# Loading w1 and w2 in chunks of 4, 4, 4 and 2 tiles, and a residual add with a choice of engine, in a fused scan and MLP kernel

## The chip, the core and the metric

The kernel runs on one core of a Trainium2 chip. The metric is the device time of one execution in microseconds (us), lower is better. A core has five engines that matter here: TensorE (PE in the profile; PEld is its weight load), VectorE (DVE), ScalarE (ACT), GpSimd (POOL) and SyncE (SP), which in this kernel issues nearly all transfers between the chip's main memory (DRAM) and the on-chip memory (SBUF). TensorE writes its products into PSUM, which has eight banks. Each engine works through its own list of instructions in order and waits on semaphores for the others.

## The reference, cut to what matters

One sequence of 2048 rows with 448 channels goes through a layer norm, a diagonal complex linear recurrence over time ("A"), and beside it through a small MLP with a hidden width of F = 1792 ("B"). The MLP's output gates the recurrence, and x is added at the end.

```python
def _A_ref(x, Lambda_re, Lambda_im, B_re, B_im, C_re, C_im, log_dt, Dskip):
    ...
    Lam_bar = jnp.exp(dt * Lam)
    Bu = jnp.einsum("bld,pd->blp", x + 0j, B_bar)
    for t in range(L):
        h = Lam_bar[None, :] * h + Bu[:, t, :]
        hs.append(h)
    hseq = jnp.stack(hs, 1)
    return 2.0 * jnp.einsum("blp,dp->bld", hseq, Cmat).real + x * Dskip[None, None, :]

def _B_ref(x, w1, b1, w2, b2):
    y = _layernorm(x, axis=-1)
    h = _gelu(jnp.einsum("bsd,df->bsf", y, w1) + b1)
    return jnp.einsum("bsf,fd->bsd", h, w2) + b2

x = A_x
xn = _layernorm(x, axis=-1)
s = _A_ref(xn, ...)
g = _silu(_B_ref(xn, B_w1, B_b1, B_w2, B_b2))
return x + s * g
```

All inputs and the output are bf16.

## The kernel before

The rows of x come in 8 blocks of 256 rows (even and odd rows of a block side by side, `par` 0 and 1), two blocks to a group, four groups. The recurrence is worked out on pairs of rows, with a scan on VectorE. For each group TensorE does: products with B (`bu`, L613), with w1 (`mm1`, L683; for the first group in halves of 256 columns, `mm1_half`, L699), with w2 (`mm2`, L714), and with C (`ym`, L746, L749 and L752). Small products (`m0`, L602 and L604) prepare a matrix once. The layer norm of a group is worked out by VectorE and either GpSimd or VectorE, and its result is transposed by DMA (`xnT` for the recurrence, `xn2T` for the MLP); only the first group's MLP input is transposed on TensorE (L379, L437).

The program is a list of tasks with what each reads and writes. Two lists of numbers fix the order in which the tasks are emitted, and which tasks with a choice of two engines take the second. Both lists were made beforehand; the kernel holds only their result.

```python
ORDER = [int(k) for k in """
0 11 18 22 12 1 9 10 19 23 14 83 16 20 24 17 2 15 5 21 25 13 27 3 26 7 8 85 6 28 4 86 29 91 40 87 30 92 84 88 93 31 89 41 94 32 43 42 44 90 48 97 95
# ... cut: 625 numbers in all
""".split()]
SECOND = [int(k) for k in """
138 141 142 143 167 171 173 197 199 217 223 284 311 318 320 393 395 396 421 422 424 425 428 503 505 506 507 532 534 535 538 541 603
""".split()]
```

The loads, issued by SyncE in this order (L84 is the helper's line):

```python
NW1 = 2

def ldw1(c, prio):
    w = F // NW1
    ld("sp", w1_sb[:, 0:3, c * w:(c + 1) * w],
       dram_ap(B_w1, c * w, [[F, 128], [128 * F, 3], [1, w]]), [f"w1_{c}"], 384 * w * 2, prio, dur=0.55)
    ld("sp", w1_sb[0:64, 3, c * w:(c + 1) * w], dram_ap(B_w1, 384 * F + c * w, [[F, 64], [1, w]]),
       [f"w1r_{c}"], 64 * w * 2, prio)

for par in range(2):
    ld("sp", x_all[:, 0, par, :], ...)             # x block 0
ldw1(0, S1 + 1)
ldx(1, 1, S1 + 2)                                   # x block 1
ld("sp", w1_sb[64:65, 3, :], dram_ap(B_b1, 0, [[F, 1], [1, F]]), ["w1b"], 4000, S1 + 1)
ldw1(1, S1 + 3)
# ... cut: B_re and B_im
for q in range(2):
    ld("sp", w2_sb[:, q * 7:q * 7 + 7, :],
       dram_ap(B_w2, q * 7 * 128 * D, [[7 * D, 128], [D, 7], [1, D]]), [f"w2_{q}"], 650000, S1 + 6, dur=1.7)
ldx(2, 2, S1 + 7)                                   # x blocks 2 and 3
# ... cut: C_im and C_re follow, then transposes of B, xn and C by DMA
```

A row of w2 on a partition holds 7 rows of DRAM that follow each other, so a tile of F takes every seventh column of w1 (`fcol`):

```python
def fcol(fi):
    q, t = divmod(fi, 7)
    return slice(q * 896 + t, q * 896 + 896, 7)

def mm1_half(j, b, k3, prio):
    # ... two tiles of F (2j, 2j+1), four matmuls of 256 columns each; cut
    w = F // NW1
    ws = sorted({(2 * j * 128) // w, ((2 * j + 2) * 128 - 1) // w})
    pe(fns, (["xmT0p0", "xmT0p1"] if b == 0 else ["xmT0_1"]) + [f"w1_{c}" for c in ws] + [f"w1r_{c}" for c in ws] + ["w1b"], ...)
    act(... ACT.Gelu_apprx_tanh ...)
```

The end of a block (`ym`): the product goes into a PSUM bank, VectorE multiplies it by the gate (L755) and adds the residual (L758), and SyncE stores it. For the last block and `par` 1, the 448 columns are done in two parts, of 256 and 192.

```python
def part(c0, c1):
    # ... matmuls into psum bank bk; cut
    dve(lambda e: e.tensor_tensor(t3[:, fb, c0:c1], psum[:, bk, c0:c1], g_sb[:, gs, c0:c1], ALU.mult), ...)
    res = xr[:, b, c0:c1] if par else x_all[:, 2 * g + b, 0, c0:c1]
    dve(lambda e: e.tensor_tensor(o_sb[:, ob, par * D + c0:par * D + c1], t3[:, fb, c0:c1], res, ALU.add), ...)
    if last:
        kb.dma("sp", ...)
for c0, c1 in ((0, 256), (256, D)) if last and par else ((0, D),):
    part(c0, c1)
```

`xr` is x plus the D skip term times the gate; it is prepared by `skip` (L730 on GpSimd, L731 on VectorE: `xd` = xn times the D skip vector `dbc`, then `xr` = `xd` times the gate, then `xr` plus x). `o_sb` shares its memory with `tmp`, and the profile calls it `tmp`.

Of the kernel before, what the change touches and what calls it, by code (L numbers as in the profile page):

```python
# [8 lines left out]
ALU = mybir.AluOpType  # L9
# [130 lines left out]
def dram_ap(t, offset, ap):  # L140
    return bass.AP(tensor=t.tensor, offset=offset, ap=ap)
# [5 lines left out]
0 11 18 22 12 1 9 10 19 23 14 83 16 20 24 17 2 15 5 21 25 13 27 3 26 7 8 85 6 28 4 86 29 91 40 87 30 92 84 88 93 31 89 41 94 32 43 42 44 90 48 97 95  # L147
45 33 49 47 96 50 34 59 99 108 46 51 100 110 57 109 101 102 98 35 103 52 112 58 111 53 114 113 39 137 104 116 115 105 176 140 136 106 60 117 138 55 61
118 56 139 107 177 54 141 62 120 175 146 63 119 148 67 163 64 122 142 164 65 144 68 121 161 124 69 66 147 123 71 149 126 77 150 125 81 70 152 143 128
78 154 72 74 127 153 130 73 151 129 79 36 162 132 131 303 82 155 134 75 302 76 178 266 80 307 133 305 135 309 165 167 304 145 308 306 168 310 270 179  # L150
267 156 166 171 181 169 157 172 274 180 158 170 37 314 311 315 271 316 159 312 227 160 313 278 268 38 183 272 269 282 228 275 173 273 182 285 229 317
279 318 186 174 283 280 362 230 281 184 392 320 284 231 363 321 188 286 276 364 185 232 287 277 235 319 233 365 236 366 187 234 395 237 322 368 245
367 241 189 191 243 370 369 244 192 193 323 240 371 194 195 372 197 413 324 415 374 419 417 373 196 199 200 325 375 412 416 414 203 380 418 198 420
326 204 201 238 215 239 327 202 246 213 216 205 248 421 422 328 376 424 425 219 430 206 220 255 223 256 431 257 329 214 258 259 207 381 330 224 388
377 382 208 427 383 378 242 428 379 249 247 209 250 426 389 251 252 217 253 390 384 218 254 423 210 260 221 261 222 211 262 225 472 332 212 226 474
263 473 264 385 265 331 386 288 475 333 338 476 336 334 341 478 477 289 335 342 480 479 339 340 344 482 387 337 481 391 345 291 346 343 290 347 348
349 484 350 483 292 429 293 351 393 295 352 485 356 502 357 394 294 490 296 190 358 353 354 355 359 360 297 298 491 492 486 299 361 432 523 522 526
527 525 398 487 529 488 524 528 489 433 530 399 493 494 300 434 396 505 400 397 531 534 535 401 495 536 532 496 540 435 402 541 403 405 503 404 436
497 504 537 301 538 437 406 539 600 408 438 407 441 439 542 442 498 440 533 443 446 543 450 447 449 570 544 451 448 545 571 499 455 456 444 457 453
445 458 572 452 459 460 409 546 467 574 461 573 410 462 463 466 464 454 465 547 468 575 469 576 411 470 548 471 500 552 578 577 551 553 549 579 556  # L160
580 550 561 558 582 581 554 555 559 508 501 583 562 560 564 584 557 509 563 510 506 603 511 566 585 588 512 586 513 587 507 565 515 567 568 592 589
514 569 590 516 517 591 596 593 601 594 602 595 518 597 598 609 519 599 606 520 610 521 604 611 613 605 607 608 612 617 614 621 615 618 616 619 622
620 623 624
""".split()]
SECOND = [int(k) for k in """
138 141 142 143 167 171 173 197 199 217 223 284 311 318 320 393 395 396 421 422 424 425 428 503 505 506 507 532 534 535 538 541 603
# [12 lines left out]
def bass_recurrent_scan__ssm_conv_s5__mixer_channel_mlp__prompt_kernel(  # L179
# [18 lines left out]
    with ExitStack() as es:  # L198
# [75 lines left out]
        with nc.Block():  # L274
# [28 lines left out]
            def ld(eng, o, i, writes, nbytes, prio, reads=(), dur=0.45):  # L303
                kb.dma(eng, o, i, reads=reads, writes=writes, prio=prio, nbytes=nbytes, dur=dur)
# [8 lines left out]
            NW1 = 2  # L313

            def ldw1(c, prio):
                w = F // NW1
                ld("sp", w1_sb[:, 0:3, c * w:(c + 1) * w],
                   dram_ap(B_w1, c * w, [[F, 128], [128 * F, 3], [1, w]]), [f"w1_{c}"], 384 * w * 2, prio, dur=0.55)
                ld("sp", w1_sb[0:64, 3, c * w:(c + 1) * w], dram_ap(B_w1, 384 * F + c * w, [[F, 64], [1, w]]),
                   [f"w1r_{c}"], 64 * w * 2, prio)  # L320
# [7 lines left out]
            ldw1(1, S1 + 3)  # L328
# [4 lines left out]
            for q in range(2):  # L333
                ld("sp", w2_sb[:, q * 7:q * 7 + 7, :],
                   dram_ap(B_w2, q * 7 * 128 * D, [[7 * D, 128], [D, 7], [1, D]]), [f"w2_{q}"], 650000, S1 + 6, dur=1.7)
# [13 lines left out]
            def xk(b):  # L349
                return [f"x{b}"] if b else ["x0p0", "x0p1"]  # L350
# [323 lines left out]
            def fcol(fi):  # L674

                q, t = divmod(fi, 7)
                return slice(q * 896 + t, q * 896 + 896, 7)

            def mm1(g, j, prio):
# [6 lines left out]
                w = F // NW1  # L686
                cs = sorted({(2 * j * 128) // w, ((2 * j + 2) * 128 - 1) // w})
# [5 lines left out]
            def mm1_half(j, b, k3, prio):  # L693
# [9 lines left out]
                w = F // NW1  # L703
                ws = sorted({(2 * j * 128) // w, ((2 * j + 2) * 128 - 1) // w})
# [5 lines left out]
            def mm2(g, b, par, prio):  # L710
# [5 lines left out]
                pe(fns, [f"gT{gb}_{fi}_{b}" for fi in range(NF)] + ["w2_0", "w2_1"], [f"ps{bk}"], 2.66, prio)  # L716
# [147 lines left out]
```

## Time and profile before

| | us |
|---|---|
| time, median of 3 | 161.2 |
| lowest and highest | 160.77, 161.3 |
| span of the profiled execution | 159.4 |
| TensorE busy | 151.2 |
| VectorE busy | 132.8 |
| ScalarE busy | 92.6 |
| GpSimd busy | 56.6 |

The span is the time from the first to the last instruction of the profiled execution. Busy times overlap between engines. A group of the profile is written as line, engine, operation, what is written and read; "<-" at a gap names what ended the engine's wait. A landing is counted from the issue of a DMA to the semaphore that tells of its end. The mean granted TensorE clock was 0.998 of full speed.

### The profile page before, as it was taken

To read this page: it belongs to the slowest core of one execution; us is meant where nothing else is said; L and a number is where in the kernel's file an instruction comes from. 1 tells how busy PE (TensorE), PEld (TensorE's weight loads), DVE (VectorE), ACT (ScalarE), POOL (GpSimd) and SP (SyncE) were. 2 spreads that over 40 slices of the span, in tenths; PEclk is the share of its full clock that TensorE was granted. 3 is DMA by queue.
4 is the path that set the end of the run, shared out by engine and by line. 5 is a ranking of instruction groups with operands and counts; after the bars stand their busy time and mean duration, and the time that the engine had idled before them with its cause. 6 is when DMAs were issued, how large, how long until landed. Compare 5 with 4: busy or idle time off the path is not lost.

```text
span 159.4 us, 2700 instructions
## 1 busy us (share of the span) xinstructions
PE 151.2 (95%) x944; PEld 97.3 (61%) x944; DVE 132.8 (83%) x254; ACT 92.6 (58%) x152; POOL 56.6 (36%) x132
## 2 busy tenths in 40 slices
PE   6689999998899999999999999999999999999990
PEld 6589965665566665546565556566677655555550
DVE  5588898468999798799984999997989899896763
ACT  3769899959895984956388211344279678111100
POOL 5568948298000622300021934632046000005230
PEclk9999999999999999999999999999999999999999
DMA  4999999995870006000001720063601000010122
GB/s 94 340 306 388 274 202 198 160 192 107 158 176 4 0 0 132 4 0 0 0 0 38 192 54 10 0 181 63 118 4 58 0 4 0 19 39 0 38 77 60
DMA packets 29926, 14.70 MB, mean 92 GB/s; under 512 B 24597, under 2 KB 29593, under 8 KB 29914
## 3 DMA queue, kind: packets, MB, share of 16 engines
q1 hardware_dynamic: 29810, 14.31, 39.5%
q0 software_dynamic: 96, 0.23, 0.4%
q8 instruction: 7, 0.11, 0.3%
q14 instruction: 5, 0.04, 0.1%
q10 hardware_dynamic: 8, 0.00, 0.0%
HBM read 6.89 MB, written 1.84 MB: 55 GB/s over the span
## 4 chain that ended last, share of the span: by engine, by line
PE 72%; DMA 10%; SPq 4%; DVE 4%; POOL 4%; ACT 2%; issue 1%; DVEq 0%; ACTq 0%; POOLq 0%
PE psum L683 21%; PE psum L714 20%; PE psum L613 12%; PE psum L746 12%; DMA x_all<-in_A_x_dram 7%; SPq L84 4%; PE psum L749 4%; PE psum L602 3%; DMA dbc<-in_A_Dskip_dram 3%; DVE lnst L357 1%; POOL lnw L400 1%; POOL dbc L338 1%; DVE t L755 1%; PE psum L752 1%; POOL xd L730 1%
## 5 line engine op out<-in xcount | busy, mean ns | idle before, releaser
L714 PE MATMUL psum<-w_sb,gT 128*128 128x448 bf16 x224 | 44.5, 352 | 0.0
L683 PE MATMUL psum<-xn2T,w_sb 128*128 128x512 bf16 x168 | 38.1, 379 | 0.0
L714 PEld LDWEIGHTS psum<-w_sb,gT 128*128 128x128 bf16 x224 | 21.8, 98 | 19.4
L683 PEld LDWEIGHTS psum<-xn2T,w_sb 128*128 128x128 bf16 x168 | 21.8, 132 | 12.9 <-issue 0.2
L690 ACT ACTIVATE gT<-psum 128x1024 bf16<-128x1024 f32 x21 | 21.5, 1023 | 11.8 <-PE psum L683 11.6
L613 PE MATMUL psum<-xnT,BT 128*128 128x256 bf16 x196 | 24.0, 273 | 1.0 <-ACT u_sb L617 1.0
L613 PEld LDWEIGHTS psum<-xnT,BT 128*128 128x128 bf16 x196 | 19.0, 98 | 6.3 <-issue 2.0
L718 ACT ACTIVATE th<-o 128x448 f32<-128x448 f32 x16 | 9.1, 573 | 20.6 <-DVE o L717 20.5
L755 DVE TENSOR_TENSOR t<-psum,g_sb 128x448 bf16<-128x448 f32 (+2 forms) x17 | 10.1, 592 | 5.7 <-PE psum L752 3.9
L638 DVE TENSOR_TENSOR_SCAN s_f<-cw,cur,v_sb 128x256 f32<-128x256 f32 x21 | 14.4, 736 | 0.2
L719 DVE SCALAR_TENSOR_TENSOR g_sb<-th,o 128x448 bf16<-128x448 f32 x16 | 10.9, 682 | 4.4 <-ACT th L718 4.4
L699 PE MATMUL psum<-xn2T,w_sb 128*128 128x256 bf16 x112 | 12.8, 273 | 1.7 <-DMA w_sb<-in_B_w_dram 1.2
L699 PEld LDWEIGHTS psum<-xn2T,w_sb 128*128 128x128 bf16 x112 | 12.1, 132 | 2.0 <-DMA w_sb<-in_B_b_dram 1.4
L730 POOL TENSOR_TENSOR xr<-xd,g_sb 128x448 f32<-128x448 bf16 x4 | 4.5, 1119 | 24.8 <-DVE g_sb L719 20.9
L421 DVE TENSOR_SCALAR xn_sb<-x_all,lnw 128x448 bf16<-128x448 bf16 x20 | 10.3, 531 | 2.0 <-POOL xd L730 1.3
L746 PE MATMUL psum<-CZ,h_sb 128*128 128x448 bf16 x56 | 11.9, 352 | 0.0
L717 DVE TENSOR_TENSOR o<-psum,b2bc 128x448 f32<-128x448 f32 x16 | 9.9, 617 | 1.6 <-PE psum L714 1.5
L617 ACT ACTIVATE u_sb<-psum 128x512 bf16<-128x512 f32 x12 | 7.1, 592 | 6.8 <-PE psum L613 3.7
L746 PE MATMUL psum<-CQ,h_sb 128*128 128x448 bf16 (+2 forms) x54 | 10.5, 332 | 0.0
L422 ACT ACTIVATE xn_sb<-x_all,lnw 128x448 bf16<-128x448 bf16 x10 | 7.5, 755 | 4.4 <-DVE xn_sb L421 3.4
L706 ACT ACTIVATE gT<-psum 128x512 bf16<-128x512 f32 x14 | 8.1, 594 | 2.6 <-PE psum L699 2.6
L357 DVE BATCH_NORM_STATS2 lnst<-x_all 128x6 f32<-128x448 bf16 x14 | 8.2, 610 | 1.6 <-DMA x_all<-in_A_x_dram 1.6
(154 smaller groups left out, 221.5 us busy)
## 6 DMA issues: line engine op xcount, KB each, us to landing
w_sb<-in_B_w_dram SPq DMA_DIRECT2D x2, 784.0 KB, 8.9
out_dram<-tmp SPq DMA_DIRECT2D x7, 224.0 KB, 2.0
w_sb<-in_B_w_dram SPq DMA_DIRECT2D x2, 672.0 KB, 5.7
x_all<-in_A_x_dram SPq DMA_DIRECT2D x3, 448.0 KB, 3.8
gT<-in_A_C_re_dram SPq DMA_DIRECT2D x1, 392.0 KB, 12.1
Bn<-in_A_B_re_dram SPq DMA_DIRECT2D x1, 336.0 KB, 6.9
Bn<-in_A_B_im_dram SPq DMA_DIRECT2D x1, 336.0 KB, 7.0
gT<-in_A_C_im_dram SPq DMA_DIRECT2D x1, 336.0 KB, 12.3
```

The lines of the kernel that those rows point to most:

```text
L357: dve([lambda e, b=b, par=par, q=q: e.bn_stats(lnst[:, q, :], x_all[:, 2 * g + b, par, :])], [f"x{2 * g + b}"] + (["xmT0p1"] if (g, b) == ...
L421: on = [("dve", lambda e: e.tensor_scalar(dst, src, rs, nb, op0=ALU.mult, op1=ALU.add), 0.4, 0.12), ("act", lambda e: e.activation(dst, sr ...
L613: fns = [lambda e, r=r, m=m, d=d: e.matmul(psum[:, 4, r * NK:(r + 1) * NK], BT[:, m, d, :], xnT[:, gx, d, :], start=(d == 0), stop=(d == 6 ...
L638: dve(lambda e, i=i, ri=ri, init=init: e.tensor_tensor_scan(s_f[:, i, ri, :], col(R2, i).to_broadcast([128, NK]), v_sb[:, i, ri, :], init, ...
L683: fns = [lambda e, k=k, d=d: e.matmul(psum[:, b0 + k, :], w1_sb[:, d, fcol(2 * j + k)], rhs[:, d, :, :], start=(d == 0), stop=(d == 3)) fo ...
L690: act(lambda e: e.activation(gT[:, gb, 2 * j:2 * j + 2, :], psum[:, b0:b0 + 2, :], ACT.Gelu_apprx_tanh), [f"ps{b0}", f"ps{b0 + 1}"] + (WK ...
L699: fns = [lambda e, k=k, d=d: e.matmul(psum[:, banks[k], :].rearrange("p (r c) -> p r c", r=2)[:, :, cs], w1_sb[:, d, fcol(2 * j + k)], rhs ...
L714: fns = [lambda e, fi=fi: e.matmul(psum[:, bk, 0:D], gT[:, gb, fi, q * 128:(q + 1) * 128], w2_sb[:, fi, :], start=(fi == 0), stop=(fi == N ...
L717: dve(lambda e: e.tensor_tensor(o2[:, fb, :], psum[:, bk, 0:D], b2bc[:], ALU.add), [f"ps{bk}", "b2bc"], [f"oo{fb}"], 0.62, prio - 76)
L719: dve(lambda e: e.scalar_tensor_tensor(out=g_sb[:, gs, :], in0=th[:, fb, :], scalar=1.0, in1=o2[:, fb, :], op0=ALU.add, op1=ALU.mult), [f" ...
L746: fns = [lambda e, k=k: e.matmul(psum[:, bk, c0:c1], h_sb[:, hb, k, k0:k0 + 128], cm[:, k, c0:c1], start=(k == 0), stop=False) for k in ra ...
L755: dve(lambda e: e.tensor_tensor(t3[:, fb, c0:c1], psum[:, bk, c0:c1], g_sb[:, gs, c0:c1], ALU.mult), [f"ps{bk}", f"g{gs}"], [f"t3{fb}_{c0} ...
```

## The change

Weights: w1 and w2 are loaded in four chunks of 4, 4, 4 and 2 tiles of F (512, 512, 512 and 256 columns of w1) in place of two of 7 tiles. The first products with w1 then wait for a smaller load, and x block 1 comes behind a smaller first chunk. Pairs of F tiles no longer straddle two chunks. The column stride in `fcol` becomes 4, and 2 in the last chunk. In the end of the last block with `par` 1, the residual add may go to VectorE or GpSimd, and the part from column 256 on no longer stands in for a dependence of the first part. Both lists of order are new; of the choices, the layer-norm scale of the second group moves from GpSimd to VectorE, and the add of the last 192 columns goes to GpSimd.

```diff
 ORDER = [int(k) for k in """
# ... cut: all 625 numbers replaced by 631
 SECOND = [int(k) for k in """
-138 141 142 143 167 171 173 197 199 217 223 284 311 318 320 393 395 396 421 422 424 425 428 503 505 506 507 532 534 535 538 541 603
+146 169 171 173 177 201 203 219 225 231 291 316 317 324 326 327 398 427 433 434 436 437 537 540 541 543 608 629

-            NW1 = 2
+            CH = ((0, 4), (4, 4), (8, 4), (12, 2))
+            chunk = [c for c, (_, n) in enumerate(CH) for _ in range(n)]
             def ldw1(c, prio):
# ... cut: the same two loads, with a, w = CH[c][0] * 128, CH[c][1] * 128
             ldw1(0, S1 + 1)
             ldx(1, 1, S1 + 2)
             ld("sp", w1_sb[64:65, 3, :], dram_ap(B_b1, 0, [[F, 1], [1, F]]), ["w1b"], 4000, S1 + 1)
-            ldw1(1, S1 + 3)
+            for c in (1, 2, 3):
+                ldw1(c, S1 + 3)
# ... cut
-            for q in range(2):
-                ld("sp", w2_sb[:, q * 7:q * 7 + 7, :],
-                   dram_ap(B_w2, q * 7 * 128 * D, [[7 * D, 128], [D, 7], [1, D]]), [f"w2_{q}"], 650000, S1 + 6, dur=1.7)
+            for c, (a, n) in enumerate(CH):
+                ld("sp", w2_sb[:, a:a + n, :], dram_ap(B_w2, a * 128 * D, [[n * D, 128], [D, n], [1, D]]), [f"w2_{c}"], 98000 * n, S1 + 6, dur=0.5 + 0.1 * n)
# ... cut
-                q, t = divmod(fi, 7)
-                return slice(q * 896 + t, q * 896 + 896, 7)
+                a, n = CH[chunk[fi]]
+                return slice(a * 128 + fi - a, (a + n) * 128, n)
# ... cut: mm1 and mm1_half
-                w = F // NW1
-                cs = sorted({(2 * j * 128) // w, ((2 * j + 2) * 128 - 1) // w})
+                cs = [chunk[2 * j]]
# ... cut: mm2
-                pe(fns, [f"gT{gb}_{fi}_{b}" for fi in range(NF)] + ["w2_0", "w2_1"], [f"ps{bk}"], 2.66, prio)
+                pe(fns, [f"gT{gb}_{fi}_{b}" for fi in range(NF)] + [f"w2_{c}" for c in range(4)], [f"ps{bk}"], 2.66, prio)
# ... cut: ym
-                    dve(lambda e: e.tensor_tensor(o_sb[:, ob, par * D + c0:par * D + c1], t3[:, fb, c0:c1], res, ALU.add),
-                        [f"t3{fb}_{c0}", f"t3{fb}_256"] + ([f"xr{b}"] if par else xk(2 * g + b)), [f"o{ob}_{par}_{c0}"], 0.1 + (0.28, 0.47)[par] * w / D, prio)
+                    add = lambda e: e.tensor_tensor(o_sb[:, ob, par * D + c0:par * D + c1], t3[:, fb, c0:c1], res, ALU.add)
+                    rd = [f"t3{fb}_{c0}", f"t3{fb}_256"] if c0 == 0 and not (last and par) else [f"t3{fb}_{c0}"]
+                    rd += [f"xr{b}"] if par else xk(2 * g + b)
+                    on = [("dve", add, 0.1 + (0.28, 0.47)[par] * w / D, 0.12), ("pool", add, 0.2 + 1.1 * w / D, 0.15)]
+                    if last and par:
+                        kb.either(*on, rd, [f"o{ob}_{par}_{c0}"], prio)
+                    else:
+                        dve(add, rd, [f"o{ob}_{par}_{c0}"], on[0][2], prio)
```

The new order also puts the 192-column part ahead of the 256-column part at the end, moves the load of b2 to an early place in GpSimd's list, and has the first two transposes of B ahead of those of xn.

## The prediction

> **What bounds the kernel now.** I read the page's busy times and slices first, then the table of windows over five stretches, then the waits of TensorE alone, then the timelines of the first 24 us and of the tail.
>
> ```profile
> PE 151.2 (95%) x944; PEld 97.3 (61%) x944; DVE 132.8 (83%) x254; ACT 92.6 (58%) x152; POOL 56.6 (36%) x132
> ...
> PE   6689999998899999999999999999999999999990
> ...
> DMA  4999999995870006000001720063601000010122
> ```
>
> TensorE is busy for 151.2 of the 159.4 us of the span. The change doesn't remove a matmul, so all that it can win lies in the other 8.2 us. The DMA row shows where loading matters: full for the first 32 us, nearly idle later. The table of windows says where the 8.2 us are (columns: stretch, length, then busy time and instruction count of each engine, clock, DMA share, GB/s):
>
> ```profile
> 0.00:8.00 8.00, 5.30 (x58) 4.85 (x59) 4.32 (x13) 4.50 (x12) 4.55 (x28) 1.00 0.76 218
> 8.00:21.00 13.00, 12.54 (x119) 12.20 (x118) 11.34 (x35) 10.92 (x21) 10.62 (x39) 1.00 1.18 315
> 21.00:42.00 21.00, 20.05 (x124) 12.45 (x123) 16.14 (x30) 18.57 (x27) 12.40 (x14) 1.00 0.99 165
> 42.00:150.00 108.00, 108.00 (x616) 64.69 (x615) 95.90 (x169) 58.63 (x94) 26.73 (x50) 1.00 0.19 44
> 150.00:159.40 9.40, 5.27 (x35) 3.14 (x33) 5.15 (x11) 0.00 (x0) 2.33 (x2) 0.97 0.22 74
> ```
>
> Length less the first busy figure gives TensorE's idle time: 2.70, 0.46, 0.95, 0.00 and 4.13 us. From 42 to 150 us there is no gap at all. The chain of waits names x_all's load, its statistics and GpSimd's steps as if they held the start; but TensorE has work meanwhile, so I don't count that chain as time to be won. Who ended TensorE's gaps:
>
> ```profile
> PE psum L699 <- DMA w_sb<-in_B_w_dram: 1.2, 1, 1.2
> PE psum L613 <- ACT u_sb L617: 1.0, 2, 0.5
> PE psum L699 <- issue: 0.5, 1, 0.5
> ```
>
> and where they lie in time:
>
> ```profile
> 5.62 0.61 PE L379 MATMUL psum<-ident,xn_sb 128*128 128x128 bf16 x8
> 7.45 2.80 PE L699 MATMUL psum<-xn2T,w_sb 128*128 128x256 bf16 x24 [1.22 <-DMA w_sb<-in_B_w_dram]
> 10.72 1.93 PE L699 MATMUL psum<-xn2T,w_sb 128*128 128x256 bf16 x16 [0.46 <-issue]
> 12.49 0.61 PE L437 MATMUL psum<-ident,xn_sb 128*128 128x128 bf16 x8
> ```
>
> The first matmul against w1 waits for the first half of w1; the fourth pair of F tiles needs both halves, and the weight load in front of it waits for the second. So the "issue" gap of 0.46 us is also a wait for w1. The DMA view, asked for the issues at 1.7 us and at 3.7 us, gives the landings:
>
> ```profile
> w_sb<-in_B_w_dram SPq DMA_DIRECT2D x1, 112.0 KB, 5.1
> ```
>
> for the first half (issued at 2.19, so landed at 7.3) and 6.4 us for the second (issued at 4.20, landed at 10.6). In the tail VectorE runs alone:
>
> ```profile
> 154.04 0.62 DVE L755 TENSOR_TENSOR t<-psum,g_sb 128x448 bf16<-128x448 f32 x1 [1.10 <-PE psum L749]
> ...
> 154.77 0.39 DVE L758 TENSOR_TENSOR tmp<-t,x_all 128x448 bf16<-128x448 bf16 x1
> 155.08 0.42 DVE L755 TENSOR_TENSOR t<-psum,g_sb 128x256 bf16<-128x256 f32 x1
> 155.53 0.43 DVE L758 TENSOR_TENSOR tmp<-t,xr 128x256 bf16<-128x256 bf16 x1
> 155.99 0.36 DVE L755 TENSOR_TENSOR t<-psum,g_sb 128x192 bf16<-128x192 f32 x1
> 156.38 0.36 DVE L758 TENSOR_TENSOR tmp<-t,xr 128x192 bf16<-128x192 bf16 x1
> ```
>
> Six VectorE steps from 154.04 to 156.74, then the last store.
>
> **What the Trainium skill says.** "DMA: Bandwidth & Descriptors", section Specifications, gives 512 B as the least transfer at line rate. The rows of the new w1 chunks are 1024 B, those of the last chunk 512 B, before they were 1792 B; so none falls under the limit. This trace has no 1024 B rows: it can't be checked before. "GPSIMD Engine Reference", section 4.1 Engine selection, says that an elementwise operation with two inputs is about twice as slow on GpSimd as on VectorE, and that GpSimd has no way to PSUM. The trace agrees with the first: GpSimd's xr multiply (L730, 448 columns) takes 1119 ns, VectorE's (L731) 623 ns. It fits the second that only the residual add, which reads SBUF alone, gets the choice.
>
> **The change, part by part.**
>
> *First matmul.* Chunk 0 of w1 is 384 + 64 = 448 KB in place of 784 KB. Between the landings at 7.3 and 10.6 us there came 784 KB of w1 and 224 KB of x: 1008 KB in 3.3 us, 305 KB a us. So 336 KB less is 1.1 us, and chunk 0 lands near 6.2. Then another wait ends last: the second copy of the transposed x (L381, two copies of 0.76 us together) ends at 6.81. With the 0.1 us that such a hand-over takes in the tail, TensorE starts near 6.95 in place of 7.45: **-0.5 us**.
>
> *Second wait for w1.* x block 1 (224 KB) follows chunk 0: 7.7 less 1.1 is 6.6. Chunk 1 (448 KB) comes 1.5 us later at 8.1, chunk 2 at 9.5, chunk 3 (224 KB) at 10.3. A pair of F tiles is 8 matmuls of 109 ns (72 of them in 7.86 us after 12.94), 0.875 us. TensorE needs chunk 1 at 6.95 + 1.75 = 8.7, chunk 2 at 10.45, chunk 3 after 12. Each is there, with 0.6 us to spare at the tightest: **-0.45 us**. The normalized block 1 has to be ready for its transposes after five pairs, at 11.3: VectorE's chain from the landing of x to the second scaling takes 4.26 us (7.71 to 11.97), and from 6.81 it ends at 11.1. Just in time.
>
> *The queue.* Six more issues of about 0.5 us on SyncE put later loads back by 3 us. But the load of x blocks 2 and 3, issued at 8.39, landed 11.7 us later behind full DMA engines; it waits for bandwidth and not for its issue. Shorter rows cost a little bandwidth; I take 0 to 0.4 us, a guess, which enters below with the transposes queued behind the loads. w2 landed at 17.8 and is needed at 19.85: hidden.
>
> *21 to 42 us.* The order on the engines changes too. Before, two TensorE gaps (0.54 and 0.41) come from ScalarE evicting u behind xn, which waits for VectorE's xn, which waits for GpSimd's xd, which waits for the D skip vector: its load is issued at 27.0, after GpSimd's power chain (23.34 to 27.0). Now the second group's scale is worked out by VectorE (ten small steps; the same ten took 2.0 us at 9.12) and GpSimd issues both vector loads earlier. These gaps should go. Against that, TensorE comes 0.95 us earlier to work that needs transposes which can't come earlier: those of xn2 landed at 33.5, and TensorE needed them at 34.45; now it needs them at 33.5, and the queue, one transpose each 1.3 us, gives them at 33.5 to 33.9. Also the first Gelu of the second group stands behind the third eviction of u and a table load of 1.28 us, which I work out to about 0.4 us of waiting for its PSUM banks. New gaps of about 0.7 for 0.95: **-0.25 us**.
>
> *The tail.* The last piece is now 256 columns and the 192-column add goes to GpSimd. On VectorE one step of 0.36 and its 0.03 gap go; the last store is 64 KB in place of 48, 1.6 us to landing in place of 1.5. GpSimd's add, 1.03 us x 192/448 with some start, about 0.5 us, ends before VectorE's last step: **-0.3 us**.
>
> Sum: -1.5 us. I give back 0.2 for the stretch from 42 us on, where the shuffled order can bring a gap that wasn't there: 161.2 - 1.3 = **159.9 us**.
>
> **The rivals.**
>
> *A. Given back by 42 us.* TensorE comes earlier and meets transposes that are no earlier; all 0.95 us won at the start turn into a wait for xn2T or BT. For: only 0.9 us of slack at 34.45, and the transposes queue one by one. Against: GpSimd's long chain is gone ahead of them. Only the tail would be left: 160.9.
>
> *B. Smaller rows or more issues hurt.* If 1024 B rows moved as slowly as the 896 B rows of B and C (VectorE and TensorE see about 250 to 275 GB/s there against 345), w1 takes 0.8 us longer and the transposes follow by as much: 161.0 to 161.6.
>
> *C. The new order stalls in the middle.* Between 42 and 150 us there is no gap now, so a new order can only be equal or worse there. Slack before the first product with CZ (75.41) is 1.9 us against VectorE's last h step (73.51). In the new order the transposes for the third group are issued only about one product with w2 and one with M0 (2.65 + 1.4 us) ahead of their use, against landings of 3.2 us. A miss would cost 0.5 to 2 us: 160.5 to 162.
>
> *D. More is won.* If no new gap comes, start, middle and tail give 0.95 + 0.95 + 0.3: 159.0.
>
> **Range and chances.** A and B put 1 to 1.5 us on top, C up to 2, D takes 0.9 off. 158.6 to 161.6 should hold it 8 times in 10. Faster by over 2% needs 3.2 us, and the idle time that loading and the last adds own is 1.2 + 0.5 + 1.0 + 0.4 = 3.1 us: hardly possible, 4%. Slower by over 2% needs a miss of more than 4 us against my sum, in an order that keeps every engine's load: 5%. Within 2%: 91%.
>
> **What would show it.** Right: the first L699 group at 6.9 to 7.1 with no second gap; the products with w2 start near 19.85 in place of 20.80; TensorE's idle time from 21 to 42 is 0.4 to 1.0 us; none from 42 on; the last VectorE step ends 2.4 us after the last even product in place of 2.8. Wrong: gaps of TensorE ended by xn2T, BT or h after 28 us, or chunk 1 landing after 8.7.

## The result, and the profile after

The changed kernel takes 163.04 us (median of 4, 162.84 to 163.59) against 161.25 beside it: a ratio of 1.0116 with a 95% interval of 1.0076 to 1.0156. A second, longer series (22 runs) gave 1.0062, 1.0040 to 1.0083. So it is slower by 0.6 to 1.2%, where 0.8% faster was predicted. The profiled span is 161.7 us against 159.4.

The page of the changed kernel, its busy times and the slices of TensorE and of the transfers (full for the first 32 us, as before):

```profile
PE 152.2 (94%) x944; PEld 93.9 (58%) x944; DVE 133.9 (83%) x254; ACT 94.8 (59%) x155; POOL 58.1 (36%) x134
...
PE   6899999795899999999999999999999999999990
...
DMA  4999999698872000380002016180330000010111
```

In TensorE's row the 7, 5 and 8 among the nines are the slices from 28 to 32 and from 36 to 44 us, where before there were 9, 8 and 8. The table of windows of the changed kernel, over the same five stretches (columns as before: length, busy time and count of PE, PEld, DVE, ACT and POOL, clock, DMA share, GB/s):

```profile
0.00:8.00 8.00, 5.85 (x60) 5.40 (x61) 4.74 (x14) 4.50 (x12) 4.55 (x28) 1.00 0.70 187
8.00:21.00 13.00, 12.98 (x121) 12.15 (x119) 10.42 (x33) 11.34 (x24) 11.06 (x39) 1.00 1.09 321
21.00:42.00 21.00, 18.20 (x111) 10.65 (x110) 17.92 (x40) 15.15 (x22) 7.35 (x9) 1.00 1.00 161
42.00:150.00 108.00, 107.27 (x612) 61.21 (x611) 94.87 (x158) 63.26 (x99) 32.48 (x58) 1.00 0.21 46
150.00:161.70 11.70, 7.92 (x49) 4.48 (x47) 5.95 (x12) 0.58 (x1) 2.62 (x3) 1.00 0.17 60
```

TensorE's idle time is now 2.15, 0.02, 2.80, 0.73 and 3.78 us. Up to 21 us it has less idle time than before, by 0.99 us together; from 21 to 42 us it has 1.85 more, and from 42 to 150 us 0.73 where there was none. Its busy time is 1.0 us longer with the same 944 matmuls, so a part of the loss is in no gap. Read the last column of the first row too: 187 GB/s, where the kernel before moved 218. In the first 8 us the transfers are slower.

Who ended TensorE's gaps in the changed kernel (us in total, times, longest):

```profile
PE psum L613 <- DMA BT<-Bn: 1.7, 1, 1.7
...
PE psum L712 <- DVE o L715: 0.9, 1, 0.9
PE psum L698 <- issue: 0.7, 1, 0.7
PE psum L683 <- ACT gT L689: 0.5, 1, 0.5
```

No gap for w1 is left, but there is one of 1.7 us for the transposed B matrix. Its timeline at the start:

```profile
5.97 0.68 PE L379 MATMUL psum<-ident,xn_sb 128*128 128x128 bf16 x8
7.32 1.91 PE L698 MATMUL psum<-xn2T,w_sb 128*128 128x256 bf16 x16 [0.67 <-issue]
```

and between the products with w2 and the second group:

```profile
30.75 2.81 PE L712 MATMUL psum<-w_sb,gT 128*128 128x448 bf16 x14 [0.86 <-DVE o L715]
33.78 1.69 PE L613 MATMUL psum<-xnT,BT 128*128 128x256 bf16 x14 [0.23 <-PE psum L712]
35.30 1.89 PE L683 MATMUL psum<-xn2T,w_sb 128*128 128x512 bf16 x8
38.91 1.69 PE L613 MATMUL psum<-xnT,BT 128*128 128x256 bf16 x14 [1.71 <-DMA BT<-Bn]
...
43.62 2.57 PE L683 MATMUL psum<-xn2T,w_sb 128*128 128x512 bf16 x11 [0.54 <-ACT gT L689]
```

The first product with w2 starts at 20.21 (before 20.80), so the change is 0.6 us ahead there. The last line's product started at 41.46 before: at 43.62 the change is 2.16 us behind. Nearly all of the loss is made between 20 and 44 us. The queue of SyncE says why B comes late (start, length of the issues):

```profile
30.09 2.62 SPq L83 DMA_TRANSPOSE xn2T<-xn_sb  x2
32.75 3.47 SPq L83 DMA_TRANSPOSE BT<-Bn  x2
```

SyncE issues in order. The two transposes of B stand behind those of xn2, which were issued at 27.92 and 29.19 before; and xn2 needs x blocks 2 and 3. Their load landed at 20.11 before and lands at 21.72 now. The four transposes are issued 1.9 to 2.2 us later. The two of B also take longer: 4.4 and 4.65 us to landing, where before they took 3.3 and 3.4. So of the 3.2 us by which the second of them is late (38.77 against 35.60), about 1.3 are made behind its issue.

The same kernel was profiled a second time (162.08 us, span 160.0). There x blocks 2 and 3 land at 20.35, only 0.24 us later than before, the wait for B is 1.0 us, and the start differs too:

```profile
6.86 1.91 PE L698 MATMUL psum<-xn2T,w_sb 128*128 128x256 bf16 x16 [0.67 <-issue]
9.24 2.81 PE L698 MATMUL psum<-xn2T,w_sb 128*128 128x256 bf16 x24 [0.47 <-DMA w_sb<-in_B_w_dram]
```

Single profiles of one kernel thus differ by 1.4 us in the landing of x; a landing that is given below for one profile carries that spread. The tail of the changed kernel (VectorE and GpSimd):

```profile
156.62 1.00 DVE L753 TENSOR_TENSOR t<-psum,g_sb 128x448 bf16<-128x448 f32 x2 [0.80 <-PE psum L747]
...
157.84 0.55 POOL L756 TENSOR_TENSOR tmp<-t,xr 128x192 bf16<-128x192 bf16 x1 [5.25 <-DVE t L753]
157.96 0.42 DVE L753 TENSOR_TENSOR t<-psum,g_sb 128x256 bf16<-128x256 f32 x1
158.42 0.42 DVE L756 TENSOR_TENSOR tmp<-t,xr 128x256 bf16<-128x256 bf16 x1
```

GpSimd's add lies beside VectorE's next multiply. The last VectorE step ends at 158.84, 2.22 us after VectorE began with the last even product (156.62); before it was 2.70 (154.04 to 156.74).

### The profile page after: what moved, and what is told of

Read it like the earlier page. It is cut to its first block, busy times and chain, and to the rows that moved or that the text cites. A ratio compares the mean times of both kernels' runs of the same rounds, so it can differ in the third digit from the quotient of the medians.

```text
span 161.7 us, 2712 instructions
## 1 busy us (share of the span) xinstructions
PE 152.2 (94%) x944; PEld 93.9 (58%) x944; DVE 133.9 (83%) x254; ACT 94.8 (59%) x155; POOL 58.1 (36%) x134
## 4 chain that ended last, share of the span: by engine, by line
PE 68%; DMA 12%; DVE 8%; SPq 6%; ACT 2%; issue 1%; POOLq 0%; DVEq 0%
PE psum L683 19%; PE psum L712 18%; PE psum L744 11%; PE psum L613 11%; DMA x_all<-in_A_x_dram 6%; SPq L84 6%; PE psum L747 4%; PE psum L602 3%; DMA BT<-Bn 3%; DMA xnT<-xn_sb 3%; DVE Bn L566 1%; DVE lnst L357 1%; DVE xn_sb L421 1%; PE psum L750 1%; ACT L689 1%
## 5 line engine op out<-in xcount | busy, mean ns | idle before, releaser
L683 PE MATMUL psum<-xn2T,w_sb 128*128 128x512 bf16 x168 | 38.8, 379 | 0.5 <-ACT gT L689 0.5
L712 PEld LDWEIGHTS psum<-w_sb,gT 128*128 128x128 bf16 x224 | 21.8, 98 | 21.0 <-PE psum L613 1.1
L689 ACT ACTIVATE gT<-psum 128x1024 bf16<-128x1024 f32 x21 | 21.3, 1021 | 12.8 <-PE psum L683 12.7
L683 PEld LDWEIGHTS psum<-xn2T,w_sb 128*128 128x128 bf16 x168 | 18.4, 112 | 16.3 <-ACT gT L689 0.8
L728 POOL TENSOR_TENSOR xr<-xd,g_sb 128x448 f32<-128x448 bf16 x8 | 9.4, 1174 | 47.4 <-DVE tmp L756 32.4
L638 DVE TENSOR_TENSOR_SCAN s_f<-cw,cur,v_sb 128x256 f32<-128x256 f32 x21 | 15.4, 770 | 0.4
L717 DVE SCALAR_TENSOR_TENSOR g_sb<-th,o 128x448 bf16<-128x448 f32 x16 | 11.7, 734 | 2.6 <-ACT th L716 2.5
L422 ACT ACTIVATE xn_sb<-x_all,lnw 128x448 bf16<-128x448 bf16 x14 | 10.6, 754 | 4.1 <-DVE lnw L408 2.6
L698 PEld LDWEIGHTS psum<-xn2T,w_sb 128*128 128x128 bf16 x112 | 11.9, 112 | 1.3 <-issue 0.8
L728 POOL TENSOR_TENSOR xr<-x_all,xr 128x448 f32<-128x448 bf16 x7 | 8.5, 1216 | 0.5
```

The lines of the kernel that those rows point to most:

```text
L422: ("act", lambda e: e.activation(dst, src, ACT.Identity, bias=nb, scale=rs), 0.75, 0.2)]
L638: dve(lambda e, i=i, ri=ri, init=init: e.tensor_tensor_scan(s_f[:, i, ri, :], col(R2, i).to_broadcast([128, NK]), v_sb[:, i, ri, :], init, ...
L683: fns = [lambda e, k=k, d=d: e.matmul(psum[:, b0 + k, :], w1_sb[:, d, fcol(2 * j + k)], rhs[:, d, :, :], start=(d == 0), stop=(d == 3)) fo ...
L689: act(lambda e: e.activation(gT[:, gb, 2 * j:2 * j + 2, :], psum[:, b0:b0 + 2, :], ACT.Gelu_apprx_tanh), [f"ps{b0}", f"ps{b0 + 1}"] + (WK ...
L698: fns = [lambda e, k=k, d=d: e.matmul(psum[:, banks[k], :].rearrange("p (r c) -> p r c", r=2)[:, :, cs], w1_sb[:, d, fcol(2 * j + k)], rhs ...
L712: fns = [lambda e, fi=fi: e.matmul(psum[:, bk, 0:D], gT[:, gb, fi, q * 128:(q + 1) * 128], w2_sb[:, fi, :], start=(fi == 0), stop=(fi == N ...
```

## The experiments

The change has three parts: chunked loads, a new order on the engines, and the tail. Theory 1 says that the chunked loads make x blocks 2 and 3 land late; theory 2, that the new order stalls by itself. "The order of before" below means that only the named part is taken from the change. Each ratio is to the kernel before, run beside it.

**The new order and tail, without the chunks.**

```diff
-CH = ((0, 4), (4, 4), (8, 4), (12, 2))      # changed kernel
+CH = ((0, 7), (7, 7))                       # w1 and w2 in halves, as before
```

> The changed kernel with its new order and tail kept, but w1 and w2 loaded in two halves of 7 tiles as before (six load issues fewer). Theory 1 (loads): the stalls between 28 and 43 us come from x blocks 2 and 3 landing late (21.7 us in the changed kernel, 20.1 before) because of the chunked loads. Then x lands by 20.5, the 1.7 us wait for the transposed B goes to under 0.4 us, the first product with w1 falls back to 7.4 to 7.5 with its second wait, and the time is 161.0 to 161.6. Theory 2 (order): the new order stalls by itself. Then x lands early too, but TensorE still waits 1.2 us or more at the third product with B, and the time is 163.0 to 163.6.

Measured: 1.0034 (1.0006 to 1.0062), x at 20.04. The wait for B is gone; one of 1.2 us for ScalarE's Gelu at 41.3 has come, larger than the 0.54 of the changed kernel. So the new order has a stall of its own.

**The chunks alone, in the order of before.**

```diff
-NW1 = 2                                     # kernel before
+CH = ((0, 4), (4, 4), (8, 4), (12, 2))      # extra loads right behind the second of each
```

> The kernel before with its own order and tail, but with the loads of w1 and w2 in chunks of 4, 4, 4 and 2. Theory 1 (loads): x blocks 2 and 3 land at 21.3 to 22 us, the first product with w1 starts at 6.9 to 7.3 without a second wait, and TensorE gets new gaps of 1.5 to 2.5 us in all between 28 and 43 us: 161.8 to 162.6. Theory 2 (order): the gaps stay near 1.0 us, the start's 0.6 us is kept: 160.5 to 160.8.

Measured: 1.0214 (1.0145 to 1.0283), x at 21.68. A second series gave 1.0190 (1.0147 to 1.0233):

> The kernel before with all loads of w1 and w2 in four chunks, a second time, on the chip of the following three. If the parts really do not add (a threshold): again 1.015 to 1.025. If the first value was too high by the few executions behind it: 1.006 to 1.013, near the sum of the parts.

So the chunks alone cost more than the whole change, and the order and tail without them cost 0.3%. Theory 2 doesn't explain the whole loss. But it isn't nothing: of the 0.6 to 1.2% of the changed kernel, 0.3% is there without the chunks.

**Group 2's scale on GpSimd again, in the changed kernel.** In the changed kernel VectorE works it out (26.12 to 29.20).

```diff
 SECOND = ...
-... 231 291 316 317 324 ...
+... 231 291 317 324 ...
```

> The changed kernel, but the layer-norm scale of the second group goes back to GpSimd (one number fewer in the list of choices). Theory 1 (loads): GpSimd's chain of 3.7 us is no shorter than VectorE's of 3.1, so xn2's transposes are issued at the same time or up to 1 us later; the wait of the second product with w2 for VectorE (0.9 us) goes, the wait for transposed B stays at 1.5 us or more: 162.5 to 163.3. Theory 2 in the form that the scale on VectorE is the cause: both waits go, 160.5 to 161.3.

Measured: 1.0197 (1.0127 to 1.0266). The scale on VectorE is no cause: without it the time is longer. Theory 1 had the signs wrong, though. In this profile x landed at 20.42, not late, and the wait for transposed B was gone; TensorE waited behind u's eviction (1.1 us), for PSUM (0.9) and for ScalarE's Gelu (1.4). A time this long without a late x shows that the place of GpSimd's steps counts as well.

**The tail alone, in the order of before.** The two parts of the last block and the choice of engine come from the change.

> The kernel before with the tail of the change alone: the 192 columns first and their add on GpSimd. All theories: VectorE's last step ends 2.3 us after the last even product in place of 2.8, and 0.2 to 0.4 us of it reach the end: 160.8 to 161.0.

Measured: 0.9981 (0.9952 to 1.0011). In its tail the 192-column add is gone from VectorE, as in the changed kernel; a gain of 0.3 us fits but isn't clear of the spread.

**Number of issues, or shorter rows?** The kernel before with six loads of 64 B more, four of them behind the second half of w1:

```diff
 ldw1(1, S1 + 3)
+for k in range(4): ld("sp", tiny[:, k, :], ...)     # 64 B each; two more behind w2
```

> The kernel before with six more load issues on SyncE of 64 B each, four behind the second half of w1 and two behind w2, which nothing waits for. No row of w1 or w2 is shorter. Theory 1a (it is the number of issues: each holds SyncE for about 0.5 us, and the transfer queue runs dry): x blocks 2 and 3 land at 21.0 to 22, time 162.2 to 164.5, which is most of what the chunked loads cost in this order. Theory 1b (it is the shorter rows): x lands at 20.0 to 20.4 and the time is the one before within 0.3%.

Measured: 1.0049 (1.0024 to 1.0074), x at 19.23, thus not later. Behind a full queue six issues do not put back this load, and cost a quarter of what the chunks cost. And the kernel before with w2 in rows of 896 B in place of 6272 B, with no issue more:

```diff
-w2_sb = SB("w2_sb", [128, NF, D])
+w2_sb = SB("w2_sb", [128, NF, D + 4])       # a gap behind each row of 448 columns
```

> The kernel before with the same issues, but w2 in rows of 896 B in place of 6272 B (a gap of 4 elements behind each row of 448 in SBUF). Theory 1a (issues): at most a small effect through the longer transfer. By packets of 34 ns worth (239 for 6272 B) against about 45 for 896 B, w2 takes 1.2 us longer and x lands 1 us later. Theory 1b (rows, and any delay of x is passed on to TensorE): x at 21.1 to 21.5 and the time 162.2 to 163.5. If x lands late and the time stays within 0.3% of before, then the landing of x isn't what costs time.

Measured: 1.0070 (1.0044 to 1.0096), x at 21.47 in one of its longer executions (164.12 us). Rows seven times shorter cost 0.7%; the chunks' w2 rows are 3584 B. Here x lands as late as in the changed kernel, as expected, and 1.4 us of delay go with a loss of 1.1 us. Neither of the two edits by itself gives the 2% of the chunks.

**Chunks at the head, but no issue more.** w1 in 4, 4 and 6 tiles with its last 64 rows in one load, w2 in 12 and 2 tiles; once in the order of before, once in the changed kernel.

```diff
-    ld("sp", w1_sb[0:64, 3, a:a + w], dram_ap(B_w1, 384 * F + a, ...))    # per chunk
+    if c == 0: ld("sp", w1_sb[0:64, 3, :], dram_ap(B_w1, 384 * F, [[F, 64], [1, F]]))
```

> The kernel before, its order and tail, with w1 in three stages (4, 4 and 6 tiles, the last 64 rows of w1 in one load of their own behind the first stage) and w2 in two (12 and 2 tiles in the rows of the changed kernel): one issue more and one less than the kernel before, so the same number, with rows nearly as short as in the changed kernel. Theory 1a (issues): x lands by 20.4, the first product with w1 starts by 7.2 without a second wait over 0.2 us, gaps between 28 and 43 us of 1.0 us at most: 160.6 to 161.3. Theory 1b (rows): x at 21 or later, 162 to 163.

> The changed kernel, its order and tail, with the loads of the run before this one. Theory 1a (issues): x by 20.4, the wait for transposed B under 0.4 us, no second wait for w1: 160.3 to 161.2. Theory 1b (rows): x at 21 or later, 162.3 to 163.3. If the waits stay though x lands early, it is the order.

Measured: 0.9991 (0.9957 to 1.0025) and 1.0018 (0.9993 to 1.0042). By the time the loss is gone in both, with the first 384 rows of chunk 0 as small as in the change (the last rows, 224 KB in one load, land 0.8 to 1.6 us after the change's 5.80). The signs expected did not come: x landed at 20.67 and at 21.32, and in the changed order TensorE still waited 1.07 us for B and 1.2 us for w1. So the ratios say that these loads cost nothing, and the landing of x in the profile doesn't say why.

**Which of the loads?** Only w1 in four chunks (four issues more), and only w2 in four (two more, w1 as in the pair above), in the order of before:

> The kernel before with its own order and tail; w1 alone comes in four chunks (eight loads in place of four, so four issues more at the head of the queue), w2 in two loads of 12 and 2 tiles. With w1 in three loads and its last rows in one, and the same w2 loads, the ratio was 0.999; with w1 and w2 both in four chunks it was 1.021. Theory 1h (small loads at the HEAD of the queue leave it too little data while the next are being issued, so all that follows lands later): nearly the whole loss is here, ratio 1.013 to 1.022, second x block after 21.3 us. Theory 1w (it is the w2 chunks, whose issues stand right ahead of what the transposes need): ratio 0.998 to 1.006, x block at about 20.5 us. Between 1.006 and 1.013: both have a part.

> The counterpart: w1 in three loads and its last rows in one, as in the kernel of the same number of issues, and only w2 in four chunks (two issues more, in the middle of the queue, with shorter rows). Theory 1h: the queue is full there, so the two issues cost little, ratio 0.998 to 1.004. Theory 1w: 1.008 to 1.02. If this kernel and the one with w1 alone in chunks both show under 0.006, the two losses don't add and a threshold (the slack of the transposed copies) decides.

Measured: 1.0063 (1.0038 to 1.0088) and 0.9996 (0.9974 to 1.0019). w2's chunks cost nothing alone; but w1's alone cost about a third of both together, so the parts don't add. Then only the last 64 rows of w1 in one load (edit as above), with all four chunks of its first 384 rows and of w2 kept, in both orders; and the changed kernel with w2 in two loads:

> The changed kernel, with one edit: the last 64 rows of w1 come in one load instead of four, so three of its six extra issues are gone, while the chunks of 4, 4, 4 and 2 tiles of w1 and w2 stay. The changed kernel is at 1.012, the changed kernel without all six extra issues at 1.002. Theory 1a (it is the issues): half of the loss goes, 1.004 to 1.008, 161.9 to 162.5 us. Theory 1b (short rows and small chunks, whatever the number of issues): 1.010 to 1.014. If the small loads of the last rows (64 partitions only) are what leaves the queue short of data: under 1.004.

> The same, with the last 64 rows of w1 in one load in place of four (three extra issues and three loads of short rows on 64 partitions fewer); the four chunks of w1's first 384 rows and of w2 stay. Theory 1r (the small loads of the last rows cost most): 1.000 to 1.005, second x block before 20.9 us. Theory 1t (threshold by the sum of all issues): half of the loss of the unmerged kernel on the same chip stays, 1.006 to 1.012.

> The changed kernel with its eight loads of w1, but w2 in two loads of 12 and 2 tiles (two issues fewer, rows of 3584 B as in the chunks). Theory 1r: the loss of the changed kernel stays, 1.009 to 1.014. Theory 1t: it falls to 1.003 to 1.007, as both w1 and w2 chunks are needed to delay the x block.

> The changed kernel itself, unedited, beside the other three: 1.010 to 1.015 under every theory; it is here to read the others against it on one chip.

Measured: 1.0035 (1.0008 to 1.0061), 1.0000 (0.9974 to 1.0026), 1.0086 (1.0052 to 1.0121) and 1.0062 (1.0040 to 1.0083). In the order of before, merging four small loads into one takes the whole 1.9% away; in the changed kernel it takes 0.3 to 0.8%, with intervals that overlap for the smaller figure, and thinning out w2's loads takes none. In the order of before thinning out w2's loads takes 1.3 of the 1.9%. So the small loads of w1's last 64 rows are needed for the loss, but don't make the whole of it alone. Who ended TensorE's gaps, in the kernel of four chunks (second series):

```profile
PE psum L698 <- DMA xn2T<-xn_sb: 2.2, 2, 1.4
PE psum L628 <- ACT u_sb L632: 1.7, 1, 1.7
...
PE psum L628 <- PE psum L698: 0.5, 1, 0.5
```

and with the last rows merged:

```profile
PE psum L723 <- DVE xn2T L406: 0.6, 1, 0.6
PE psum L638 <- issue: 0.4, 1, 0.4
```

The waits for transposed copies are gone. A part of that is TensorE's own lateness in this profile: from 8 to 11 us it started 17 products where it started 27 with four chunks (15 to 19 in the profiles of three other kernels too; the granted clock reads 1.00 in all), and it came to w2 at 21.78 in place of 20.50. Why is not known. But the transposes of xn2 were issued at 28.59 in place of 29.43, and the span is 3.9 us shorter all the same.

Not all of those 3.9 us belong to the head. The second wait for xn2T in the kernel of four chunks lies far behind all loads of weights:

```profile
119.12 1.89 PE L698 MATMUL psum<-xn2T,w_sb 128*128 128x512 bf16 x8 [1.42 <-DMA xn2T<-xn_sb]
```

All three profiles with four chunks in the order of before have it (1.0, 1.4 and 1.2 us), no other has it. The transpose took 4.5 to 4.9 us to landing there, and 3.1 or 3.2 in the nine other profiles in this order. By the packet records of this profile one 16 KB packet of the queue that the page calls instruction (q8) runs from 116.99 to 117.93; the last two semaphore writes of the transpose come at 117.92 and 117.93, the other 30 of them had come by 116.75. In the other two profiles such a packet (116.28 to 117.24, 116.04 to 116.92) also lies ahead of two late writes (118.00 and 117.56). In the kernel with w2 alone in chunks the packet starts at 115.90, just behind the last semaphore write. In the changed kernel such a packet (34.60 to 35.78) overlaps the transposes of B that landed late. No run moves this packet by itself, so the collision is read from the traces and not tested. 1.0 to 1.4 us are 0.6 to 0.9% of the time, and fit a good part of what the two kinds of chunks cost together beyond their sum (1.3 to 1.5%).

What happens in the queue can be read from the window 4 to 6 us (the last two columns are the transfers' busy share and GB/s). First the kernel before:

```profile
4.00:6.00 2.00, 1.94 (x30) 1.63 (x29) 1.17 (x4) 1.66 (x10) 0.59 (x3) 1.00 1.07 367
```

the changed kernel:

```profile
4.00:6.00 2.00, 1.94 (x24) 1.63 (x22) 1.08 (x4) 1.56 (x10) 0.59 (x3) 1.00 0.90 217
```

four chunks in the order of before, second series:

```profile
4.00:6.00 2.00, 1.94 (x24) 1.63 (x23) 1.41 (x4) 1.47 (x9) 0.52 (x3) 1.00 0.87 231
```

and the same with the last rows merged:

```profile
4.00:6.00 2.00, 1.94 (x24) 1.63 (x23) 1.16 (x4) 1.63 (x10) 0.61 (x3) 1.00 1.05 273
```

A share of 0.87 to 0.90 where it was 1.05 to 1.07: the engines of the queue stand idle for part of these 2 us. In the changed kernel's packet records no row of 1024 B starts between 5.28 and 6.06; chunk 1, issued at 3.71, begins at 6.06. Ahead of it there stand 448 KB of w1 (384 and 64) and 224 KB of x; in the kernel before it is 784 KB of w1 and the same x. With the last rows in one load it is 608 KB of w1, and the engines stay busy, if with less in each us than before. The sum of rate times length over windows of 2 us gives what had been moved. The landing of x blocks 2 and 3 in the same profile stands beside it:

| kernel | w1's last rows | moved by 8 us, MB | by 18 us, MB | x lands, us | ratio |
|---|---|---|---|---|---|
| before | 2 loads of 1792 B rows | 1.74 | 5.20 | 20.1 | 1 |
| halves, changed order | 2 loads of 1792 B rows | 1.81 | 5.33 | 20.0 | 1.003 |
| w2 in rows of 896 B, order of before | 2 loads of 1792 B rows | 1.53 | 4.66 | 21.5 | 1.007 |
| no issue more, order of before | 1 load | 1.68 | 5.25 | 20.7 | 0.999 |
| no issue more, changed order | 1 load | 1.57 | 5.18 | 21.3 | 1.002 |
| only w2 in four | 1 load | 1.63 | 5.23 | 20.3 | 1.000 |
| last rows merged, order of before | 1 load | 1.64 | 5.18 | 20.7 | 1.000 |
| last rows merged, changed order | 1 load | 1.54 | 5.10 | 21.1 | 1.004 |
| only w1 in four | 4 loads | 1.51 | 4.93 | 20.2 | 1.006 |
| changed, w2 in two | 4 loads | 1.52 | 4.97 | 20.9 | 1.009 |
| changed | 4 loads | 1.49 | 4.94 | 21.7 | 1.012 |
| changed, second profile | 4 loads | 1.58 | 4.94 | 20.4 | 1.006 |
| four chunks, order of before (second series) | 4 loads | 1.50 | 4.86 | 21.8 | 1.019 |

By 18 us the four-load kernels are 0.22 to 0.34 MB behind the kernel before, about 0.6 to 1 us at its 340 to 400 GB/s; the other kernels are at most 0.1 behind, but for the one with w2 in short rows (0.54). Most of the deficit (0.16 to 0.25 MB) is there at 8 us. The kernels with one load for the last rows are behind by 0.06 to 0.2 at 8 us too, and make up most of it by 18. The four-load kernels are thus slower at the head and in the time; how much slower in the time, neither the bytes nor the landing of x tells: the kernel with the fewest bytes loses 0.7%, and x lands at 20.2 in a kernel that loses 0.6% and at 21.3 in one that loses 0.2%.

**Is the hole itself the cause?** One edit keeps all loads, rows and counts, and only takes the issue of b1's row, which stands between chunk 0 and chunk 1, off SyncE:

```diff
-ld("sp", w1_sb[64:65, 3, :], dram_ap(B_b1, 0, ...))
+ld("act", w1_sb[64:65, 3, :], dram_ap(B_b1, 0, ...))
```

> The kernel of all loads in four chunks in the order of before (1.019 and 1.021), with one edit: the issue of the bias row b1 (3.6 KB, 0.5 us of SyncE between the first and the second chunk) stands on ScalarE, behind its four small loads. Nothing else of the loads changes, so all of SyncE's later issues come 0.5 us earlier. Theory D (the dry stretch of the queue between 4.5 and 6 us is the cause): 150 to 180 KB more moved by 8 us (1.68 to 1.74 MB), ratio 1.005 to 1.013. Theory R (short rows and the number of transfers are the cause): the ratio stays at 1.016 to 1.023. A price of up to 0.2 us is possible, as ScalarE's first activation comes later.

> The same edit in the changed kernel (1.012, and 1.006 in the second series). Theory D: 1.7 MB moved by 8 us, the second w1 wait under 0.2 us, ratio 0.998 to 1.006. Theory R: 1.007 to 1.013.

Measured: 1.0142 (1.0091 to 1.0193) and 1.0043 (1.0015 to 1.0070). The edit did less than I had worked out: SyncE's next issue of x took 0.58 us in place of 0.36, so chunk 1 was issued at 3.42, 0.3 us earlier and not 0.5. By 8 us 1.61 and 1.58 MB had been moved (1.50 and 1.49 without the edit, 1.58 in the second profile of the changed kernel), by 18 us 5.02 and 4.91; x landed at 20.66 and 22.35. In the order of before the loss shrinks by a quarter to a third, for nearly half of the deficit at 8 us made up; the intervals overlap those of the unedited kernels. In the changed order the ratio is in the range that theory D (the hole) expected, but the profile shows no gain by 18 us and the latest x of all runs, so the ratio doesn't speak for theory D. The hole in the queue stays a likely cause that isn't shown.

**The version that the runs point to.** The same-issue loads in the order of before, with the new tail:

> The version that the runs so far point to: order of the kernel before, w1 in 4, 4 and 6 tiles with its last rows in one load, w2 in 12 and 2 tiles (no issue more than before), and the changed kernel's tail with the split residual add. Alone the loads gave 0.999 and the tail 0.998. If the two add up: 0.997 (160.7 to 160.9 us). If the start's gain is given back as before and the tail is noise: 1.000.

Measured: 161.08 us, 0.9974 (0.9954 to 0.9995). It is the only one faster than the kernel before by more than its interval, by 0.26%, about 0.4 us: loads and tail add up. With the same loads and the same tail, the new order gives 1.0018; with the last rows merged, the order of before gives 1.0000 without the tail and the new order 1.0035 with it. So where the loads do no harm, the new order costs about 0.4% against the old one.

## Why the prediction was wrong, step by step

- **First matmul, -0.5: mis-sized.** Chunk 0 landed at 5.80, earlier than the 6.2 worked out, but TensorE started at 7.32 in place of 6.95, so 0.13 us was won. The copy did end the wait, as foreseen, but at 7.22 and not at 6.81: the transposes of x block 0 came at 5.97 in place of 5.62, behind warm-up products that took 1.03 us in place of 0.64. In the second profile of the same kernel they came at 5.57 and TensorE started at 6.86, close to the 6.95; so the working was sound and the profiles differ.
- **Second wait, -0.45: the landing mis-sized, the gap hidden.** Chunk 1 landed at 9.2 in both profiles, not 8.1, beyond the 8.7 that I had named as the mark of being wrong. In the first profile TensorE was itself late and lost about 0.2 us to it (the product before started at 8.96, the first on chunk 1 at 9.25, with 0.11 us between products); in the second, where it started at 6.86, it waited 0.47 us. So only one of the two gains of the head came, in either profile.
- **The queue: the first step that failed.** "It waits for bandwidth and not for its issue" was true of the kernel before, where the queue was full, and I carried it into a kernel whose head is smaller. There the queue ran short between 4 and 6 us (217 GB/s in place of 367), by 18 us 0.25 MB less had been moved, and x blocks 2 and 3 landed 1.6 us later in one profile and 0.2 in the other. My sum of landings used 305 KB a us throughout, and so assumed a queue that never runs out. The guess of 0 to 0.4 us covered shorter rows. The runs show 0.3 to 0.8% (0.5 to 1.3 us) for the chunked loads in the new order and 1.9 to 2.1% in the old one, and that loss goes when the three extra small loads of w1's last rows are merged into one.
- **21 to 42 us, -0.25: the second step that failed, wrong sign, +1.85.** I saw that slack before the xn2 transposes was only 0.9 us, and that time won at the start makes TensorE meet them earlier. That was rival A; rival B's delay came on top. The kernel with chunks at the head, no issue more and the order of before shows rival A by itself: it comes to w2 at 20.18 (before 20.80), is 0.55 us behind at 42.01, and ends at 0.9991. In the changed kernel the wait that ended last was B's transpose, which stands behind xn2's on SyncE. The gaps that the new order was to remove, behind u's eviction, did go; larger ones came. Where the loads do no harm the new order is at 1.002 to 1.004 with its tail. So without the failed step of the queue the forecast 0.992 would not have come either.
- **From 42 us on, +0.2:** TensorE's idle time there is 0.73 us, 0.54 of it at 43.6, for ScalarE's Gelu, where I had worked out about 0.4. Rival C did not come at the places that I had named. From 43.6 us to the last even product another 0.4 us is lost in small pieces (2.16 behind, then 2.58).
- **Tail, -0.3: right in kind,** 0.48 us by the profile. GpSimd's add took 0.55 us as estimated, against VectorE's 0.36 before; the Trainium skill's "GPSIMD Engine Reference", section 4.1 Engine selection, says about twice, here it is 1.5. The last store's end ran 0.2 us longer behind the last step.

Sum of what was measured in the first profile: 0.6 ahead at 20 us, 2.75 lost to 43.6, 0.4 to the last product, 0.5 won and 0.2 lost in the tail: 2.3 us, the difference of the spans. In the second the spans differ by 0.6 us.

The Trainium skill's "DMA: Bandwidth & Descriptors", section Issuing engines are not separate DMA queues, calls the sequencer's time to initiate a transfer usually small relative to the transfer. Against the time to landing that holds at the head of this kernel: an issue takes SyncE 0.36 to 0.59 us, and the loads of w1 land 3.6 to 5.8 us after it. Against the time to move the bytes it doesn't: I work out 0.2 us for the 64 KB of a small load at 350 GB/s.

**What stays open.** What limits the head is not settled: SyncE's time per issue, or the rate at which rows are handed to the queue (a row of 3584 B in place of 1024 B fills more of the same time, so merging changes both). The only edit that kept the rows moved the time by 0.2 to 0.7%, mostly inside the intervals. The way from the head to the lost time is argued from single profiles: x's landing differs by 1.4 us between two profiles of one kernel. Why w1's chunks alone cost 0.6% and with w2's chunks 2%, while w2's chunks alone cost nothing, is explained in part by the wait at 119 us, if its cause is the packet of the instruction queue. The load of the D skip vector doesn't settle the rest: with four chunks in the order of before it landed 5 us after its issue in place of 4, but in the kernel with only w2 chunked it took 5.8 us, and nothing was lost.

## What to carry to other kernels

When a first load is cut into chunks, add up the bytes that stand in the queue ahead of each next chunk, and compare them with the time until that chunk's first packet; in this kernel, with 448 KB in the first chunk of w1 and a new load each half microsecond, the queue ran short, and less had been moved 14 us later. Before cutting the small remainder of a matrix along with it, try loading it once: here that was never slower. Take a second profile before you explain a landing that moved by 1 us. And time won ahead of a transfer that comes no earlier is only waited for later; look for the transfer with the least slack first.

## What was not expected of the hardware

- The time from issue to first packet isn't fixed: x block 0 was issued at 0.79 and its first packet started at 1.80 (1.0 us), chunk 1 of w1 was issued at 3.71 and began at 6.06 (2.35 us), with the queue in part idle.
- By the packet records a 1792 B row took 74 ns (24 GB/s on one engine), a 1024 B row 46 ns (22), a 512 B row 27 to 45 ns (11 to 19), a 3584 B row 140 ns (26), in the middle or for most of the rows. The Trainium skill's "DMA: Bandwidth & Descriptors", section Specifications, gives 512 B as enough for line rate; here 512 B rows move at four fifths of the rate of 1792 B rows or less.
- Six issues of 64 B, most of them behind a full queue, cost 0.5% although in the profile x blocks 2 and 3 landed no later (19.23).
- A DMA transpose took 4.5 to 4.9 us to landing in the three profiles where one 16 KB packet of another queue (0.9 to 1.0 us) ran just ahead of its last writes, and 3.1 or 3.2 us otherwise. That the packet holds it up is not tested.
